# Token rows from grouped pairs of 64-column products, tokens dealt in two halves, one table set named first, and a new written order

## The chip, the cores and the metric

The kernel runs on one NeuronCore of a Trainium2 chip. The core has five engines that work side by side: TensorE (PE, with its weight loads shown apart as PEld), VectorE (DVE), ScalarE (ACT), GpSimd (POOL) and SyncE (SP, which issues most transfers). PE writes to PSUM, which DVE and ACT read. The metric is device time in microseconds, the lower the better: the median of timed runs. The changed kernel is compared with the kernel before by such runs.

## The reference

One block of a sequential model, for 2048 tokens of 512 channels: a layer norm, a convolution along the tokens with a state-space kernel (128 complex modes for each channel), a skip, then a second layer norm pair and a two-layer perceptron.

```python
x = A_u                                    # 1 x 2048 x 512, bfloat16
h = x + A(layernorm(x))                    # mixer along the tokens
h2 = h + B(layernorm(h))                   # B norms once more, then the perceptron

# A, for each channel d:
K[d, l] = Re( sum_n C[d,n] * exp(dt[d] * A[d,n] * l) * dt[d] * B[d,n] )
y = irfft(rfft(u, 2L) * rfft(K, 2L))[:L] + u * Dskip

# B:
g = gelu(layernorm(x) @ w1 + b1)           # 512 -> 1376
return g @ w2 + b2                         # 1376 -> 512
```

## The kernel before, in words

The convolution is done by a two-step transform over the 2048 tokens (padded to twice that), written as matrix products. A token number is split into a partition p (128) and a row j (16), token = 16 p + j. The small first step (BD, line 844) goes over the partitions; its result `a` goes to DRAM (A_dram) and comes back with the axes exchanged (X). The large step is `xps` (lines 882 to 885). The kernel's spectrum `kfps` (line 930) is multiplied in by DVE (`pa`, `pb`, then X), the inverse large step is `zps` (lines 966 to 969), its result `z` is written to DRAM (Zd) and read back with axes exchanged (ZT), and the inverse small step multiplies ZT by the matrix D (`Dm` in profiles) and so makes the token rows `y`. Each half of the 512 channels (hh = 0 and 1) goes through this by itself, in eight groups k2 of frequencies.

The state-space kernel itself (`kps`) is made from exponentials (ACT, `Pt` and `Q` from `th`), sines (ACT, `s` and `sq` from PE's phases `pv` and `qv`) and their products (DVE). Its `samples` go to DRAM (`KD`, line 784) and come back as `kt` (line 794), five pieces, all of which `kfps` needs. ACT must load a table set before it can change between sines and exponentials; `logs` (line 127) names the set that has both Ln and Exp, an activation without a named set loads one by itself.

All of this is one list of operations, each with a number; `Sched.run` (line 161) goes through the table ORDER and issues them as it says, and the last two bits of an entry choose the engine where there is a choice (ACT or DVE for a copy out of PSUM, SP or POOL for a transfer). There is no planner at run time: every engine works its instructions off in the order in which they were issued, and an instruction that waits holds up all behind it on its engine, SP's and POOL's transfers too.

The token rows are made in three ways. `early_rows` (line 1132) makes the first channel half of rows j = 0 to 7: for each row an identity product that adds the residual x, then one product with D for each half h of the frequencies, 128 columns each, added in PSUM (`half_rows`, line 1110). `head_rows` (line 1020) makes the second channel half of rows 0 to 3 and takes the last frequencies directly from `z` by a widened matrix W (`yh`). In `mlp` (line 1194) `y_rows` makes rows 4 to 7 of the second half and `y_row` (line 1221) makes rows 8 to 15 with all 512 channels at once, between the up-projections of the quarter before.

`mlp` works on four quarters of four rows (512 tokens): 11 blocks of up-projection (`h1ps`, line 1260, with Gelu on ACT into hT), then `down` (line 1265): for each row 11 products into `o2ps`, one DVE addition of h into `ot`, one store. Statistics and roots of the norms are on DVE (`ve` to `r4y`). PE's PSUM here has three tags: `h1ps` (four banks), `yps` (two) and `o2ps` (two). The loads of the perceptron's weights (`late_loads`, line 1180) are issued by SP once a one-column ACT copy into their tile (line 1096) has been done.

Of the kernel before, what the change touches and what calls it, by code (L numbers as in the profile page):

```python
# [11 lines left out]
ALU = mybir.AluOpType  # L12
f32 = mybir.dt.float32
# [3 lines left out]
P = 128  # L17
# [64 lines left out]
def bc(ap, shape):  # L82
    return ap.to_broadcast(shape)

# [104 lines left out]
def prefix(nc0, S, K, cp, ct, c2):  # L189
# [41 lines left out]
    split = ((3, 15), (0, 7), (0, 1), (1, 1))  # L231
    bits = c2.tile([P, 4], i32, name="bits")
    for n, (sh, m) in enumerate(split):
        ts(nc, bits[:, n:n + 1], pi[:], sh, ALU.logical_shift_right, m, ALU.bitwise_and)
    pf = ct.tile([P, 4], f32, name="pf")
    nc.vector.tensor_copy(pf[:], bits[:])
    t1, q, odd, b1 = (pf[:, n:n + 1] for n in range(4))
# [9 lines left out]
    t1s = col(t1, 1.0 / 64, 0.0)  # L247
# [12 lines left out]
    ts(nc, mask[:], kf[:, 0:8], q, ALU.is_equal)  # L260
# [222 lines left out]
def params(nc, S, K, cp, pp, sc, cv, psp, raws, ldt, dtb, grb):  # L483
    T, S2, Z = {}, S.op, {}

    def step():
        for h in range(2):
            d = slice(HW * h, HW * h + HW)
            nc.scalar.activation(dtb[:, d].rearrange("p (j g) -> p g j", g=4), ldt[:, d].rearrange("p (g j) -> p g j", g=4), ACT.Exp)
# [530 lines left out]
def head_rows(nc, S, K, psp, cv, o_tail):  # L1020
    K.o_head = []
    for n in range(2):
# [32 lines left out]
        m = S.op("PE", 0.65, main, K.o_z[0:6] + K.o_r0[0:1] + [o_tail], acq="p")  # L1055
# [54 lines left out]
def half_rows(nc, K, out, hh, js, more=False):  # L1110
    for j in range(js.start, js.stop):
        if more:
            nc.tensor.matmul(out[:, j - js.start], lhsT=K.ident[:], rhs=K.X[:, j, hh, 0:HW], start=True, stop=False)
        for h in range(2):
            nc.tensor.matmul(out[:, j - js.start], lhsT=K.D[:, h], rhs=K.ZT[:, hh, h, j, :], start=(h == 0 and not more), stop=(h == 1))
# [16 lines left out]
def early_rows(nc, S, K, psp, z0, r0):  # L1132
    for n in range(2):
# [14 lines left out]
        m = S.op("PE", 1.35, mm, z0 + r0[n:n + 1], acq="p")  # L1148
# [41 lines left out]
def residual(q, K, xv, n):  # L1190
    q.dma_start(K.X[:, 4 * n:4 * n + 4, :, 0:HW], xv[:, 4 * n:4 * n + 4].rearrange("p j (h d) -> p j h d", h=2))


def mlp(nc, tc, K, w1, w2, b2, xv, ov):
    with tc.tile_pool(name="m_sb", bufs=1) as sb, tc.tile_pool(name="m_rot", bufs=2) as rot, tc.tile_pool(name="m_ps", bufs=2, space=PSUM) as ps1:
        hT = [sb.tile([P, NFC, 512], bf16, name=f"hT{n}") for n in range(2)]
        y2, y2T, mv, yps = {}, {}, {}, {}
# [23 lines left out]
        def y_row(tb, jj):  # L1221
            yp = yps[tb, jj] = ps1.tile([P, 1, 2, HW], f32, name="y2", tag="yps")
            for h in range(2):
                nc.tensor.matmul(yp[:, 0], lhsT=K.D[:, h], rhs=K.ZT[:, :, h, 4 * tb + jj, :], start=(h == 0), stop=(h == 1))  # L1224
# [68 lines left out]
        for fc in range(NFC):  # L1293
            up(0, fc, pairs[1])
            if fc in (1, 3):
                y_rows(1, fc // 2)
# [156 lines left out]
```

## Time and profile before

| what | value |
|---|---|
| timed runs | 261.05, 261.68, 262.22 us; median 261.68 |
| profiled execution | the page gives its span: 260.3 us |
| PE, DVE, ACT busy | 220.3, 203.3, 179.5 us |
| granted TensorE clock | 1.000 |
| moved by DMA | 33.61 MB, 129 GB/s in the mean |

The span runs from the first to the last instruction of the profiled execution; a timed run has the start and the end of the program around it. In the rows below, PE's matmuls are pipelined: one lasts longer than the step to the next, and only the step counts for a stream.

### The profile page before, as it was taken

How to read it: one execution, taken by the hardware profiler on the slowest of the kernel's cores; microseconds unless marked ns; L12 is line 12 of the kernel's file. 1: busy time of each engine (PE TensorE's matmuls, PEld its weight loads, DVE VectorE, ACT ScalarE, POOL GpSimd, SP SyncE). 2: the span in 40 equal slices, each digit the busy share in tenths (PEclk: the TensorE clock that was granted, in tenths of full speed). 3: DMA queues.
4: the chain of work that ended last, by engine and by line, in shares of the span. 5: the costliest groups of instructions: out<-in, count | busy, mean ns of one | idle time of the engine just before them, and what ended most of it. 6: DMA issues, size and time to landing. Idle time of an engine off the chain costs nothing.

```text
span 260.3 us, 4481 instructions
## 1 busy us (share of the span) xinstructions
PE 220.3 (85%) x1585; PEld 138.3 (53%) x1585; DVE 203.3 (78%) x447; ACT 179.5 (69%) x303; POOL 40.0 (15%) x104
## 2 busy tenths in 40 slices
PE   2899308765688797899999999968999999999994
PEld 2323102322276585567988888857744444444443
DVE  6999999998999999999688999975836754761022
ACT  6999999999999999998833565448604703612810
POOL 8922960000003000100560010010000000000000
PEclk9999999999999999999999999999999999999999
DMA  5802951967695910410189678969541033022001
GB/s 166 293 7 34 191 162 61 162 170 244 183 357 148 227 11 24 139 44 0 53 180 267 185 201 242 264 197 240 141 102 59 1 63 101 0 54 80 31 26 54
DMA packets 49442, 33.61 MB, mean 129 GB/s; under 512 B 22154, under 2 KB 47900, under 8 KB 49164
## 3 DMA queue, kind: packets, MB, share of 16 engines
q1 hardware_dynamic: 47676, 28.66, 41.8%
q0 software_dynamic: 1744, 4.68, 7.1%
q8 instruction: 12, 0.20, 0.3%
q14 instruction: 10, 0.08, 0.1%
HBM read 18.65 MB, written 11.26 MB: 115 GB/s over the span
## 4 chain that ended last, share of the span: by engine, by line
PE 43%; DVE 16%; ACT 6%; DMA 6%; issue 2%; POOL 0%; DVEq 0%; POOLq 0%; ACTq 0%
PE o2ps L1273 14%; PE h1ps L1260 12%; PE kfps L930 8%; DVE Pt L79 5%; DMA ZT<-Zd 4%; DVE Q L79 3%; DVE X L79 2%; PE kps L765 2%; ACT Pt L673 2%; DVE pa L79 2%; DVE pb L79 2%; ACT sq L142 2%; DMA Zd<-z 2%; DVE X L91 1%; PE y L1224 1%
## 5 line engine op out<-in xcount | busy, mean ns | idle before, releaser
L1263 ACT ACTIVATE hT<-h1ps,b_sb 128x512 bf16<-128x512 f32 (+3 forms) x55 | 31.9, 604 | 41.9 <-PE h1ps L1260 40.2
L1260 PE MATMUL h1ps<-y2T,wide 128*128 128x512 bf16 (+3 forms) x220 | 40.5, 336 | 0.6 <-DVE ve L75 0.6
L1273 PE MATMUL o2ps<-w_sb,hT 128*128 128x512 bf16 (+3 forms) x187 | 38.7, 366 | 0.0
L930 PE MATMUL kfps<-kt,M 128*128 128x256 bf16 x320 | 37.9, 273 | 0.0
L79 DVE TENSOR_TENSOR ot<-o2ps,h 128x512 bf16<-128x512 f32 (+1 forms) x17 | 11.0, 658 | 30.3 <-PE o2ps L1273 16.9
L930 PEld LDWEIGHTS <-M 128*128 128x128 bf16 x320 | 31.3, 98 | 4.9 <-issue 1.2
L1260 PEld LDWEIGHTS <-wide 128*128 128x128 bf16 (+1 forms) x220 | 21.8, 100 | 17.0 <-issue 0.8
L1273 PEld LDWEIGHTS <-hT 128*128 128x128 bf16 (+1 forms) x187 | 18.3, 98 | 19.7
L79 DVE TENSOR_TENSOR Pt<-s,Pt 128x512 bf16<-128x512 bf16 (+1 forms) x48 | 23.0, 510 | 0.9 <-ACT s L142 0.3
L844 PE MATMUL aps<-u,BD 128*128 128x512 bf16 x32 | 10.2, 407 | 15.2 <-DVE u L839 11.2
L89 ACT CAST z<-zps 128x1024 bf16<-128x1024 f32 (+1 forms) x15 | 14.8, 992 | 10.6 <-PE zps L969 10.6
L673 ACT ACTIVATE Pt<-th 128x256 bf16<-128x256 f32 x64 | 20.7, 401 | 0.0
L142 ACT ACTIVATE sq<-qv 128x1024 bf16<-128x1024 int16 x20 | 20.1, 1077 | 0.0
L142 ACT ACTIVATE s<-pv 128x1024 bf16<-128x1024 int16 x16 | 16.9, 1077 | 0.0
L89 ACT CAST a<-aps 128x1024 bf16<-128x1024 f32 x16 | 15.8, 1053 | 0.5 <-DMA A_dram<-a 0.5
L738 PE MATMUL qv<-RQ,PQ 128*128 128x512 bf16 (+1 forms) x64 | 11.6, 298 | 4.7 <-ACT a L89 1.6
L844 PEld LDWEIGHTS <-BD 128*128 128x128 bf16 x32 | 3.0, 99 | 21.6 <-DVE u L839 14.3
L91 DVE CAST X<-xps 128x1024 bf16<-128x1024 f32 x12 | 14.3, 1219 | 0.0
L79 DVE TENSOR_TENSOR h<-y,X 128x512 f32<-128x512 f32 x10 | 6.9, 686 | 8.6 <-PE y L1224 5.6
L79 DVE TENSOR_TENSOR Q<-sq,Q 128x1024 bf16<-128x1024 bf16 x20 | 13.0, 685 | 0.1
L681 ACT ACTIVATE Q<-th 128x256 bf16<-128x256 f32 x40 | 13.0, 401 | 0.0
L449 POOL DMA_DIRECT2D Dp<-Dd x24 | 11.9, 504 | 7.2 <-DMA Dd<-ds 6.9
(246 smaller groups left out, 446.9 us busy)
## 6 DMA issues: line engine op xcount, KB each, us to landing
A_dram<-a SPq DMA_DIRECT2D x16, 256.0 KB, 2.6
X<-A_dram SPq DMA_DIRECT2D x4, 1024.0 KB, 7.2
Zd<-z SPq DMA_DIRECT2D x15, 256.0 KB, 3.4
x<-in_A_u_dram SPq DMA_DIRECT2D x4, 512.0 KB, 6.9
ZT<-Zd POOLq DMA_DIRECT2D x8, 256.0 KB, 4.1
ZT<-Zd SPq DMA_DIRECT2D x8, 256.0 KB, 3.6
out_dram<-ot SPq DMA_DIRECT2D x15, 128.0 KB, 1.9
X<-in_A_u_dram SPq DMA_DIRECT2D x3, 512.0 KB
```

The costliest lines, as they stand in the source:

```text
L79: (nc.vector if e == "DVE" else nc.gpsimd).tensor_tensor(out, a, b, op)
L89: nc.scalar.copy(out, in_)
L91: nc.vector.tensor_copy(out, in_)
L142: nc.scalar.activation(out, v.bitcast(i16)[..., 0:2 * n:2], ACT.Sin, scale=S2PI / 65536)
L449: nc.gpsimd.dma_start(t[o::128 // cnt], bass.AP(row.tensor, row.offset + 1024 * kh, [[0, cnt], [1, 1024]]))
L673: nc.scalar.activation(K.Pt[:, 1, :, k, :], K.th[:, ds].rearrange("p (e g) -> p e g", g=4), ACT.Exp, scale=float(8 * k))
L681: nc.scalar.activation(K.Q[:, 1, :, m, :], K.th[:, ds].rearrange("p (e g) -> p e g", g=4), ACT.Exp, scale=float(OFFS[m]))
L844: nc.tensor.matmul(ps[:, h, :], lhsT=K.BD[:, h].rearrange("p a b -> p (a b)"), rhs=cell["u"][:], start=True, stop=True)
L930: nc.tensor.matmul(ps[:, k, c, :], lhsT=K.M[:, t, k0 + k, c, :], rhs=kt[:, t, :], start=((plain or c == 1) and t == 0), stop=(t == 4))
L1260: nc.tensor.matmul(pt[:fs, 0:n], lhsT=K.w1_sb[:, dc, fc * P:fc * P + fs], rhs=(y2T[tb][:, dc, js, :] if tb or js.start else K.y2T[:, dc]). ...
L1263: nc.scalar.activation(hT[tb % 2][:fs, fc, cols], pt[:fs, 0:n], ACT.Gelu_apprx_tanh, bias=K.b1_sb[:fs, fc:fc + 1], scale=1.0)
L1273: nc.tensor.matmul(pt[:], lhsT=h[:fs, fc, jj * P:(jj + 1) * P], rhs=K.w2_sb[:fs, fc, d], start=(fc == 0), stop=(fc == NFC - 1))
```

## The change

1. Tokens are dealt otherwise: partition 64 h + p holds the rows 32 p + 16 h + j. With the mask of the forward small step made for that, the inverse small step falls apart into two halves: output partitions 64 h to 64 h + 63 need only half h of the frequencies. So the two products with D of a row, each 128 columns wide and added up, become two of 64 columns, each into its own half of the PSUM partitions.
2. These pairs are grouped: in `half_rows` all identity products come first, then all pairs; `y_rows` and `y_row` are called once per quarter, behind the third up-block (fc == 2), for all rows. For four rows at a time, two take their PSUM from the `o2ps` tag.
3. Loads of x and stores of the result go by partition halves (more transfers of x, each half as large; stores of two rows at once, and the last stores half on ACT's queue). The residual load r0 is now by halves, so that early and head rows need both of its parts.
4. `step`, the first exponentials, calls `logs` first.
5. Four small DVE operations more at the start (three bits and one combination), for the new mask.
6. A new table ORDER.

```diff
+def half(h):
+    return slice(64 * h, 64 * h + 64)
+
+def dealt(x):
+    return x.rearrange("(p h j) d -> h p j d", h=2, j=16)
...
-    split = ((3, 15), (0, 7), (0, 1), (1, 1))
+    split = ((3, 15), (0, 7), (0, 1), (1, 1), (2, 15), (0, 3), (6, 1))
...
-    t1s = col(t1, 1.0 / 64, 0.0)
+    t1s = col(tk, 1.0 / 64, 0.0)
...
-    ts(nc, mask[:], kf[:, 0:8], q, ALU.is_equal)
+    stt(nc, tq, tq, 2.0, th, ALU.mult, ALU.add)
+    ts(nc, mask[:], kf[:, 0:8], tq, ALU.is_equal)
...
     def step():
+        logs(nc)
         for h in range(2):
...
 def half_rows(nc, K, out, hh, js, more=False):
+    for j in range(js.start, js.stop) if more else ():
+        nc.tensor.matmul(out[:, j - js.start], lhsT=K.ident[:], rhs=K.X[:, j, hh, 0:HW], start=((j - js.start) % 2 == 0), stop=False)
     for j in range(js.start, js.stop):
-        if more:
-            nc.tensor.matmul(out[:, j - js.start], lhsT=K.ident[:], rhs=K.X[:, j, hh, 0:HW], start=True, stop=False)
         for h in range(2):
-            nc.tensor.matmul(out[:, j - js.start], lhsT=K.D[:, h], rhs=K.ZT[:, hh, h, j, :], start=(h == 0 and not more), stop=(h == 1))
+            nc.tensor.matmul(out[half(h), j - js.start], lhsT=K.D[:, h, half(h)], rhs=K.ZT[:, hh, h, j, :], start=not more, stop=not more or j % 2 == 1)
...
-            yp = yps[tb, jj] = ps1.tile([P, 1, 2, HW], f32, name="y2", tag="yps")
+            yp = yps[tb, jj] = ps1.tile([P, 1, 2, HW], f32, name="y2", tag="o2ps" if jj > 1 else "yps")
             for h in range(2):
-                nc.tensor.matmul(yp[:, 0], lhsT=K.D[:, h], rhs=K.ZT[:, :, h, 4 * tb + jj, :], start=(h == 0), stop=(h == 1))
+                nc.tensor.matmul(yp[half(h), 0], lhsT=K.D[:, h, half(h)], rhs=K.ZT[:, :, h, 4 * tb + jj, :], start=True, stop=True)
...
-            if fc in (1, 3):
-                y_rows(1, fc // 2)
+            if fc == 2:
+                for n in range(2):
+                    y_rows(1, n)
...
-                    if tb < 3 and fc in (1, 3, 5, 7):
-                        y_row(tb + 1, fc // 2)
-                        sums_row(tb + 1, fc // 2)
+                    if tb < 3 and fc == 2:
+                        for jj in range(4):
+                            y_row(tb + 1, jj)
+                        for jj in range(4):
+                            sums_row(tb + 1, jj)
...
     for n in range(4):
-        nc.sync.dma_start(x[:, 4 * n:4 * n + 4], xv[:, 4 * n:4 * n + 4])
+        for h in range(2):
+            nc.sync.dma_start(x[half(h), 4 * n:4 * n + 4], xv[h, :, 4 * n:4 * n + 4])
...
+                for b in range(2) if last or r else ():
+                    q = nc.scalar if last and b else nc.sync
+                    q.dma_start(ov[b, :, j:j + 1, d] if last else ov[b, :, j - 1:j + 1, :], ot[half(b), :, d])
```

Three places of the new order. First SP's queue where the second channel half's samples go to DRAM and come back (KD_66 and kt are of that half, Zd_67 and ZT of the first half), before:

```order
L997 DMA Zd_67<-z 128x4x256 x3
L784 DMA KD_66<-samples 128x1x320 x3
L794 DMA kt<-KD_66 128x4x64
L997 DMA Zd_67<-z 128x4x256
L794 DMA kt<-KD_66 128x4x64 x3
L1015 DMA wide<-Ds 4x8x128 x4
```

and now:

```order
L1009 DMA Zd_67<-z 128x4x256 x3
L796 DMA KD_66<-samples 128x1x320 x4
L1007 DMA ZT<-Zd_67 16x8192
L1009 DMA Zd_67<-z 128x4x256
L806 DMA kt<-KD_66 128x4x64 x2
L1007 DMA ZT<-Zd_67 16x8192
L806 DMA kt<-KD_66 128x4x64 x3
L1027 DMA wide<-Ds 4x8x128 x4
```

One KD and one kt that POOL issued have come to SP, and two ZT stand between them. On PE, one group of eight zps that stood ahead of the first kfps with this kt now stands behind it.

Second, DVE at the turn into the second layer (`y_22..` are the early rows, `yh` the head rows, `y_237.` the scaled rows of which PE makes the transposed `tps`), before:

```order
L91 CAST z<-zps 128x512
L1146 BN_STATS st_1905<-y_2248 128x6 x4
L1146 BN_STATS st_1905<-y_2277 128x6 x4
L1046 BN_STATS st_1905<-yh 128x6 x2
L1053 BN_AGGR mv_1906<-st_1905 128x2 x2
L1046 BN_STATS st_1905<-yh 128x6 x2
L75 TENSOR_SCALAR y_2376<-h,mv_1906,rs_1907 128x256 x4
L91 COPY y2T_1909<-tps 128x512
```

and now:

```order
L101 CAST z<-zps 128x512
L1158 BN_STATS st_2239<-y_2254 128x6 x4
L1158 BN_STATS st_2239<-y_2285 128x6 x4
L1058 BN_STATS st_2239<-yh 128x6 x2
L1065 BN_AGGR mv_2240<-st_2239 128x2 x2
L76 TENSOR_SCALAR y_2378<-h,mv_2240,rs_2241 128x256 x4
L1058 BN_STATS st_2239<-yh 128x6 x2
L101 COPY y2T_2243<-tps 128x512 x2
```

The scaling has moved ahead of the second statistics of the head rows. The CAST is of the last `z` of all now; before it was of the last but one, and the last was on ACT.

Third, ACT at the same place, before:

```order
L1142 COPY h<-y_2248 128x4x256
L1142 COPY h<-y_2277 128x4x256
L89 CAST z<-zps 128x512
L1049 COPY h<-yh 128x2x256
L1096 CAST wide<-h 128x1
L1070 ACTIVATE rs_1907<-mv_1906,eps 128x2
L1071 ACTIVATE rs_1907<-rs_1907 128x2
```

and now:

```order
L1154 COPY h<-y_2254 128x4x256
L99 CAST z<-zps 128x512
L1154 COPY h<-y_2285 128x4x256
L1082 ACTIVATE rs_2241<-mv_2240,eps 128x2
L1083 ACTIVATE rs_2241<-rs_2241 128x2
L1061 COPY h<-yh 128x2x256
L1108 CAST wide<-h 128x1
```

The root `rs` stands ahead of the copy of h and of the one-column copy that lets the weight loads go.

More of the change, by code (lines that the diff above doesn't have):

```diff
@@ L230, in prefix @@
         at += n
-    split = ((3, 15), (0, 7), (0, 1), (1, 1))
-    bits = c2.tile([P, 4], i32, name="bits")
+    split = ((3, 15), (0, 7), (0, 1), (1, 1), (2, 15), (0, 3), (6, 1))
+    bits = c2.tile([P, 7], i32, name="bits")
     for n, (sh, m) in enumerate(split):
         ts(nc, bits[:, n:n + 1], pi[:], sh, ALU.logical_shift_right, m, ALU.bitwise_and)
-    pf = ct.tile([P, 4], f32, name="pf")
+    pf = ct.tile([P, 7], f32, name="pf")
     nc.vector.tensor_copy(pf[:], bits[:])
-    t1, q, odd, b1 = (pf[:, n:n + 1] for n in range(4))
+    t1, q, odd, b1, tk, tq, th = (pf[:, n:n + 1] for n in range(7))
     cols = ct.tile([P, 5], f32, name="cols")
@@ L1053, in total @@
                 nc.vector.bn_aggr(K.mv0[:, j, :], K.st[:, j].rearrange("p h s -> p (h s)"))
-        m = S.op("PE", 0.65, main, K.o_z[0:6] + K.o_r0[0:1] + [o_tail], acq="p")
+        m = S.op("PE", 0.65, main, K.o_z[0:6] + K.o_r0 + [o_tail], acq="p")
         i = [S.op(("PE", "NONE"), (0.65, 0.0), pause, [m, K.o_zs[5]]) for _ in range(1 + 2 * n)]
@@ L1146, in stats @@
                 nc.vector.bn_stats(K.st[:, j, 0, :], cell["y"][:, j - js.start])
-        m = S.op("PE", 1.35, mm, z0 + r0[n:n + 1], acq="p")
+        m = S.op("PE", 1.35, mm, z0 + r0, acq="p")
         s = S.op("DVE", 1.5, stats, [m], rel=[m])
@@ L1190, in residual @@
 def residual(q, K, xv, n):
-    q.dma_start(K.X[:, 4 * n:4 * n + 4, :, 0:HW], xv[:, 4 * n:4 * n + 4].rearrange("p j (h d) -> p j h d", h=2))
+    h, rows = n % 2, slice(8 * (n // 2), 8 * (n // 2) + 8)
+    q.dma_start(K.X[half(h), rows, :, 0:HW], xv[h, :, rows].rearrange("p j (c d) -> p j c d", c=2))
 def mlp(nc, tc, K, w1, w2, b2, xv, ov):
@@ L1196, in mlp @@
         hT = [sb.tile([P, NFC, 512], bf16, name=f"hT{n}") for n in range(2)]
-        y2, y2T, mv, yps = {}, {}, {}, {}
+        y2, y2T, mv, yps, ots = {}, {}, {}, {}, {}
         def root(tb, js):
@@ L1266, in down @@
             j, h = 4 * tb + jj, hT[tb % 2]
-            parts = 2 if tb == 3 and jj == 3 else 1
+            last = tb == 3 and jj > 1
+            parts = 2 if last and jj == 3 else 1
+            if last or jj % 2 == 0:
+                ots[0] = rot.tile([P, 1 if last else 2, 512], bf16, name="ot", tag="ot")
+            ot, r = ots[0], 0 if last else jj % 2
             for n in range(parts):
@@ L1273, in down @@
                     nc.tensor.matmul(pt[:], lhsT=h[:fs, fc, jj * P:(jj + 1) * P], rhs=K.w2_sb[:fs, fc, d], start=(fc == 0), stop=(fc == NFC - 1))
-                ot = rot.tile([P, 512 // parts], bf16, name="ot", tag="ot")
-                tt(nc, ot[:], pt[:], K.h[:, j, d], ALU.add)
-                nc.sync.dma_start(ov[j][:, d], ot[:])
+                tt(nc, ot[:, r, d], pt[:], K.h[:, j, d], ALU.add)
+                for b in range(2) if last or r else ():
+                    q = nc.scalar if last and b else nc.sync
+                    q.dma_start(ov[b, :, j:j + 1, d] if last else ov[b, :, j - 1:j + 1, :], ot[half(b), :, d])
         tiles(0)
@@ L1341 @@
     psp = front.enter_context(tc.tile_pool(name="ps", bufs=1, space=PSUM))
-    xv = x_dram.rearrange("(p j) d -> p j d", j=16)
+    xv = dealt(x_dram)
     early = ExitStack()
@@ L1414 @@
     S.group = None
-    r0 = K.o_r0 = [S.op(("POOL", "SP"), (0.8, 0.45), lambda e, n=n: residual(nc.gpsimd if e == "POOL" else nc.sync, K, xv, n), x0[2 * n:2 * n + 2], lat=3.0) for n in range(2)]
+    r0 = K.o_r0 = [S.op(("POOL", "SP"), (0.8, 0.45), lambda e, n=n: residual(nc.gpsimd if e == "POOL" else nc.sync, K, xv, n), x0[0:4], lat=3.0) for n in range(2)]
     K.o_early = []
@@ L1420 @@
     front.close()
-    mlp(nc, tc, K, B_w1, B_w2, B_b2, xv, out_dram.rearrange("(p j) d -> j p d", j=16))
+    mlp(nc, tc, K, B_w1, B_w2, B_b2, xv, dealt(out_dram))
     order.__exit__(None, None, None)
```

47 rows, old and new, of the table ORDER are left out of this document.

## The prediction

> **What bounds the kernel now.** I read the page's busy shares first, then the busy times in stretches, then the chain of waits in order of time, and last the timeline at the places that the change touches. The page:
>
> ```profile
> span 260.3 us, 4481 instructions
> PE 220.3 (85%) x1585; PEld 138.3 (53%) x1585; DVE 203.3 (78%) x447; ACT 179.5 (69%) x303; POOL 40.0 (15%) x104
> ```
>
> No engine is full on average, so the stages have different limits. Two stretches of 20 us (start:end, length, then busy time and count of PE, PEld, DVE, ACT, POOL, then PE clock, DMA share, GB/s):
>
> ```profile
> 100.00:120.00 20.00, 16.92 (x159) 11.63 (x157) 19.55 (x39) 19.49 (x22) 0.90 (x1) 1.00 0.23 66
> 140.00:160.00 20.00, 19.76 (x180) 17.41 (x179) 19.09 (x36) 10.52 (x12) 1.93 (x4) 1.00 0.74 215
> ```
>
> Up to about 123 us ACT and DVE are both full; afterwards PE is, with DVE close to it until 160. The chain of waits, in order of time, shows the hand-over and what holds PE later (start, length, what):
>
> ```profile
> 121.20 1.96 ACT sq L142 x2
> 123.20 1.92 PE kps L765 x48
> ...
> 172.50 9.30 DMA ZT<-Zd
> ...
> 182.45 0.87 PE h1ps L1260 x8
> ...
> 198.06 0.43 PE y L1224 x2
> 198.49 1.73 PE h1ps L1260 x8
> ```
>
> So three things count: when ACT's last sines let PE go at 123.2, whether PE waits after that, and how many streaming slots PE needs. A matmul with 256 moving columns takes 0.87/8 = 0.109 us of the stream, one with 512 takes 1.73/8 = 0.216.
>
> **Part 1, the table load and the small DVE work.** The start of the kernel:
>
> ```profile
> 2.09 0.34 DVE L180 TENSOR_SCALAR bits<-pi 128x1 int32<-128x1 int32 x4 [2.09 <-POOL pi L196]
> 3.53 0.24 ACT L142 ACTIVATE wb<-bw 128x32 bf16<-128x32 int16 x1 [1.52 <-DVE bw L180]
> 3.79 1.28 ACT L489 ACT_TABLE_LOAD   x1
> 5.08 1.34 ACT L489 ACTIVATE M<-M 128x256 bf16<-128x256 bf16 x2
> 6.44 1.28 ACT L129 ACT_TABLE_LOAD   x1
> 6.46 0.69 DVE L79 TENSOR_TENSOR th<-tps_are,M 128x512 f32<-128x512 f32 x1
> 7.74 1.33 ACT L681 ACTIVATE Q<-th 128x256 bf16<-128x256 f32 x4
> ```
>
> The change makes the load at 3.79 the logarithm's, so the one at 6.44 goes: 1.28 us less on ACT. But the next exponentials need th. Three more DVE bits (0.34/4 each, 0.25) delay wb, hence the load, the two exponentials and th, which then ends at 6.46 + 0.25 + 0.69 = 7.40. ACT gains 7.74 − 7.42 = 0.3; DVE, equally full, starts th 0.25 later. Bounds at 123 us: a loss of 0.3, if DVE alone decides, to a gain of 1.3, the whole load, if the rest of the new order removes the engines' small waits. I take **+0.5**, the middle. The four more loads of x cost SP at most four KD issues (0.74 each, part 2), and SP has nothing else to issue before 22 us, so they are hidden; without that cover it would be 3 us.
>
> **Part 2, SP's queue at 126 us.** This term speaks against the change. Second half's kernel samples go out to DRAM (KD) and come back (kt), and PE's kfps of that half need all five kt:
>
> ```profile
> 126.15 2.23 SPq L784 DMA_DIRECT2D KD<-samples  x3
> 126.42 0.57 POOL L784 DMA_DIRECT2D KD<-samples  x1 [20.09 <-DVE X L79]
> 130.91 1.68 SPq L794 DMA_DIRECT2D kt<-KD  x3
> 134.96 0.57 SPq L995 DMA_DIRECT2D ZT<-Zd  x1
> 136.77 3.00 PE L930 MATMUL kfps<-kt,M 128*128 128x256 bf16 x26
> ```
>
> By the rows for the two transfers, from issue to landing (first KD, then kt):
>
> ```profile
> DMA to landing us min/median/max: 2.3/2.3/2.3
> DMA to landing us min/median/max: 3.7/3.7/4.0
> ```
>
> Before: the last kt is issued at 130.91 + 2 × 0.56 = 132.0 and lands at 135.7, 1.1 before PE's 136.77. In the new order POOL has none of these: SP issues four KD (126.15 + 3 × 0.74: the last at 128.4, landed 130.7), a ZT and a Zd meanwhile, then two kt, a ZT, three kt at about 0.56 each: the last kt at 130.7 + 5 × 0.56 = 133.5, landed at 137.2. And PE asks sooner, for one group of eight zps (8 × 0.109 = 0.87) now stands behind the first kfps of this half: at 135.9. PE waits 1.3, and everything behind in its queue (zps, all kfps) with it; DVE and ACT wait for those. PE has no slack from there to 171 us, so it is lost: **−1.3**. Bounds: 0, if kt lands in KD's 2.3 (135.8), and worse as rival C prices it.
>
> **Part 3, the turn into the second layer.** Here the new order and the paired matmuls meet:
>
> ```profile
> 165.00 0.68 DVE L91 CAST z<-zps 128x512 bf16<-128x512 f32 x1
> 165.60 2.79 DVE L1146 BATCH_NORM_STATS2 st<-y 128x6 f32<-128x256 f32 x8
> 166.04 0.27 PE L969 MATMUL zps<-X,Rn 128*128 128x256 bf16 x1
> 166.82 0.59 ACT L89 CAST z<-zps 128x512 bf16<-128x512 f32 x1
> 170.56 0.37 SPq L1181 DMA_DIRECT2D wide<-in_B_w_dram  x1
> 171.34 0.76 DVE L1046 BATCH_NORM_STATS2 st<-yh 128x6 f32<-128x256 f32 x2 [1.41 <-PE yh L1038]
> 172.01 1.37 DVE L75 TENSOR_SCALAR y<-h,mv,rs 128x256 bf16<-128x256 f32 x4
> 174.76 3.65 PE L1260 MATMUL h1ps<-y2T,wide 128*128 128x256 bf16 x32 [0.61 <-DVE ve L75]
> 181.84 0.61 PE L1115 MATMUL y<-ZT,Dm 128*128 128x256 bf16 x4 [0.80 <-DMA ZT<-Zd]
> ```
>
> The scaling of the first two rows (172.01) no longer queues behind statistics for which DVE idled 1.41. But DVE now casts the last z before the eight statistics and waits for PE's last zps (end 166.31). Pairs at no gain: cast to 167.2, eight statistics to 170.0, two more 0.76, about 1.2 for aggregate and root: scaling at 171.9, and with 0.76 of statistics now between it and the transposed copies PE starts at 175.0, 0.2 late. Pairs at full gain (16 products in 8 slots, 0.87 earlier): PE starts at 174.1 or somewhat before, 0.7 early. I take **+0.5**, nearer the upper end, since loads fit (part 4).
>
> The PE wait of 0.80 at 181.84 was for the last ZT, which took 9.30 behind the weight loads that SP began at 170.56. Now the ACT copy that lets those go stands behind the root and a copy of h, so they start at about 171.5, while the last Zd, cast directly, goes 0.2 to 1.1 earlier than 167.41. ZT is issued first, and the products that need it are four matmuls (0.44) later in PE's order. I take the whole wait as gone, **+0.8**; kept, it is 0. What is late next is the tail of the up weights:
>
> ```profile
> wide<-in_B_w_dram SPq DMA_DIRECT2D x1, 608.0 KB, 4.3
> ```
>
> Issued at 171.5, it is there at 175.8; with PE starting at 174.3 the columns are asked for 24 matmuls (2.6) later, at 176.9. So 1.1 is in hand; if the load takes longer than 5.4, PE waits.
>
> **Part 4, the pairs.** Two 128-column products per row become two of 64 columns into separate halves of PSUM. Rows before of the products, their loads, and the only narrower load that follows the same weights:
>
> ```profile
> L1224 PE MATMUL y<-ZT,Dm 128*128 128x512 bf16 x16 | 4.8, 379 | 0.0
> L1224 PEld LDWEIGHTS <-Dm 128*128 128x128 bf16 x16 | 1.6, 98 | 1.9
> L1260 PEld LDWEIGHTS <-wide 128*96 128x96 bf16 x20 | 2.4, 123 | 1.2
> ...
> 18.20 0.63 PE L368 MATMUL v<-gb,si 1*128 1x512 bf16 x1
> 18.63 0.63 PE L368 MATMUL v<-row_k,si 1*128 1x512 bf16 x1
> 19.19 0.58 PE L625 MATMUL k<-M,ones 128*1 128x512 bf16 x1
> ```
>
> No row has 64 columns. A load of 64, scaled from the 96-column row, is about 0.082, so two (0.164) fit under one 512-column matmul (0.216). A change of column count shows once: 0.56 between 18.63 and 19.19 where 0.43 is the step, so at most 0.13, 0.26 for going in and out. A group of eight 512-column products (two groups: third and fourth quarter of the rows) costs 8 × 0.216 = 1.73 now; 4 × 0.216 + 0.26 = 1.12 if pairs overlap, 1.99 if not: +1.2 to −0.5 for both. I take **+0.9**: the loads fit and the switch price is an upper one. The 256-column group of the second quarter is bound by its loads, 4 × 0.164 + 0.26 = 0.92 against 0.87: 0, with +0.3 to −0.3 around it. The new wait, for the down-projection's PSUM in rows 3 and 4 of a group, is met by DVE while twelve up matmuls (12 × 0.216 = 2.6) run.
>
> [...]
>
> Stores: fewer, larger, and the last halves on two queues; 0, give or take 0.3.
>
> **Sum** against the profiled span: 0.5 − 1.3 + 0.5 + 0.8 + 0.9 = 1.4, so 258.9. The timed median, 261.68, lies 1.4 above the span; I carry that over: **260.3**.
>
> **Rivals.** A: kt is in time (landing in KD's time, or asked later) and pairs overlap fully: 1.0 + 0 + 0.7 + 0.8 + 1.2 = 3.7, so 258.0. For it: 1.1 us of slack before; against: the count of SP's issues. B, slower: PE runs the two halves one after the other. Then the 512 groups lose 0.5, the 256 group 0.3, the early groups, with two switches each, start the layer 0.7 late: 0.5 − 1.3 − 0.7 + 0.8 − 0.3 − 0.5 = −1.5, 263.2. It decides from a pair costing 0.43 on. For it: no row shows overlap of two matmuls; against: separate columns and separate PSUM halves. C: the ZT transfers ahead of kt hold it longer, as 9.30 shows one can be held; each 1 us beyond 137.2 is lost whole, and from 2.7 more the kernel is slower by over 0.5%. With 2 more: 262.3. Against: ZT ran beside kt before, too.
>
> **Chances.** Forecast 0.45, A 0.25, B 0.15, C 0.15. This measurement tells apart about 0.5% (1.3 us), and the forecast sits on that edge: its share is split 0.22 faster, 0.21 no change, 0.02 slower. With A all faster, B 0.04 / 0.11 and C 0.08 / 0.07 (no change / slower): faster 0.47, no change 0.33, slower 0.20. The forecast's own range is 259.3 to 261.3; the range over the cases, leaving out the far ends of A and B, is 257.6 to 262.6.
>
> **What would show it.** One table load fewer by 8 us and the first long exponentials near 7.4; a PE wait of 1 us or more ahead of the first kfps of the second half, on kt; no wait on ZT in the second layer; y products of one 512-column group within 1.1 to 1.4 us, second starts of a pair close behind the first. No wait on kt, or pairs 0.43 apart, would make the prediction wrong.

## The result

The changed kernel takes 272.6 us in the median (270.2 to 273.7), the kernel before 261.5 in the same comparison: a ratio of 1.041, with a 95% interval from 1.036 to 1.047. Forecast were 260.3 us in a range from 257.6 to 262.6. The profiled execution has a span of 270.7 us, 10.4 more than before. In experiment 2, one execution of each of the two runs lies more than 1.5% above that run's fastest and is left out of its time and ratio.

The page of the changed kernel (busy time and share by engine, then the TensorE clock in 40 slices of the span, 9 standing for 90% or more):

```profile
span 270.7 us, 4459 instructions
PE 221.6 (82%) x1570; PEld 138.1 (51%) x1583; DVE 203.2 (75%) x451; ACT 178.3 (66%) x302; POOL 35.2 (13%) x96
PEclk9999999999999979999995999979999999999999
```

PE works 1.3 us longer than before (221.6 against 220.3), some of it under a slower clock, and no other engine works longer, so nearly all of the 10 us are waits. And the clock row, all nines before, has three dents, near 98, 146 and 182 us. PE's timeline shows a wait for a transfer just ahead of each (start, length, what, and in brackets the idle time before it and what ended it):

```profile
93.60 1.54 PE L942 MATMUL kfps<-kt,M 128*128 128x256 bf16 x9 [2.72 <-DMA M<-Bd]
...
144.66 4.21 PE L942 MATMUL kfps<-kt,M 128*128 128x256 bf16 x19 [4.92 <-DMA kt<-KD]
...
178.87 0.38 PE L1043 MATMUL yh<-ZT,Dm 96*128 96x256 bf16 x2 [2.60 <-DMA ZT<-Zd]
```

The second also shows what the dent costs: 19 kfps in 4.21 us, where 20 took 2.35 before. Busy times by stretch, cut finely, give the borders of the three slow stretches (after the busy times: granted clock, DMA share, GB/s):

```profile
94.50:95.00 0.50, 0.50 (x5) 0.36 (x4) 0.50 (x2) 0.00 (x0) 0.00 (x0) 0.54 0.00 0
97.50:98.00 0.50, 0.50 (x4) 0.38 (x3) 0.00 (x0) 0.48 (x1) 0.00 (x0) 0.55 0.00 0
142.00:142.50 0.50, 0.00 (x0) 0.00 (x0) 0.50 (x2) 0.00 (x0) 0.00 (x0) 0.82 1.18 111
149.00:149.50 0.50, 0.50 (x6) 0.41 (x5) 0.50 (x1) 0.00 (x0) 0.00 (x0) 0.85 1.15 285
179.00:180.00 1.00, 1.00 (x10) 0.88 (x9) 0.00 (x0) 0.52 (x1) 0.00 (x0) 0.94 1.07 373
183.00:184.00 1.00, 1.00 (x10) 0.83 (x8) 0.64 (x4) 0.29 (x1) 0.18 (x1) 0.86 0.83 262
```

Between these borders the clock is 0.50: from 94.5 to 97.9, from 142.3 to 149.2 and from 179.9 to 183.3, that is 3.4, 6.8 and 3.4 us. In the first stretch ACT and DVE, which bound the kernel there, run dry (busy for 0.38 and 0.61 of its 3.4 us): their casts and products wait for PE's slow kfps.

**The first wait** begins in SP's queue. The last kt reads, the last transposing load R from M, and only then the two writes of the table's last row, for which the kfps wait:

```profile
85.77 2.48 SPq L806 DMA_DIRECT2D kt<-KD  x3
88.29 2.59 SPq L490 DMA_TRANSPOSE R<-M  x1
90.93 1.60 SPq L473 DMA_DIRECT2D M<-Bd  x2
```

**The second** begins on POOL, with the residual rows (`X<-in_A_u_dram`, 512 KB). From POOL's timeline, and from the transfers issued between 134 and 145 us (count, KB each, median us from issue to landing):

```profile
134.92 0.86 POOL L1204 DMA_DIRECT2D X<-in_A_u_dram  x1
```

```profile
X<-in_A_u_dram POOLq DMA_DIRECT2D x1, 512.0 KB, 9.0
kt<-KD SPq DMA_DIRECT2D x5, 64.0 KB, 8.3
```

Before, POOL issued the first residual load at 105.4, when the transfers' engines were idle (DMA share 0.00 from 105 to 105.5 us), and it landed in 5.3 us. It filled four rows and needed two products of the first half; as half loads each fills eight rows and needs four, and the fourth is done only at 124 us. POOL then has a memset and four small transfers ahead of it. So it fell among the kt reads, and the kt reads took 8.3 us instead of 3.7 to 4.0.

**The third** is the way of the last z that the head rows need. ACT's cast for it ends at 170.3; the chain of waits, in order of time, shows both transfers behind it:

```profile
170.32 3.44 DMA Zd<-z
173.77 4.85 DMA ZT<-Zd
178.63 0.25 issue
178.87 0.38 PE yh L1043 x2
```

What the change meant to do works. Groups of eight paired products of 256 and of 512 columns (chain of waits) last 0.56, 0.98 and 1.05 us:

```profile
194.21 0.56 PE y L1127 x8
...
210.47 0.98 PE y L1237 x8
...
230.50 1.05 PE y L1237 x8
```

No ZT wait stands ahead of the first of them, where 0.80 stood before. And ACT starts its long exponentials with one load less, at 7.19 instead of 7.74:

```profile
3.79 1.28 ACT L139 ACT_TABLE_LOAD   x1
5.08 1.35 ACT L501 ACTIVATE M<-M 128x256 bf16<-128x256 bf16 x2
7.19 1.95 ACT L685 ACTIVATE Pt<-th 128x256 bf16<-128x256 f32 x6 [0.76 <-DVE th L80]
```

### The profile page after: what moved, and what is told of

It is laid out like the page before. It is cut to its first block, busy times and chain, and to the rows that moved or that the text cites. A ratio compares the mean times of both kernels' runs of the same rounds, so it can differ in the third digit from the quotient of the medians.

```text
span 270.7 us, 4459 instructions
## 1 busy us (share of the span) xinstructions
PE 221.6 (82%) x1570; PEld 138.1 (51%) x1583; DVE 203.2 (75%) x451; ACT 178.3 (66%) x302; POOL 35.2 (13%) x96
## 4 chain that ended last, share of the span: by engine, by line
PE 45%; ACT 19%; DVE 15%; DMA 13%; issue 4%; SPq 3%; POOL 1%; DVEq 0%; ACTq 0%; POOLq 0%
PE o2ps L1290 14%; PE h1ps L1273 13%; PE kfps L942 9%; DMA X<-A_dram 4%; DVE Pt L80 3%; DMA kt<-KD 3%; ACT s L152 2%; ACT a L99 2%; ACT sq L152 2%; ACT Q L693 2%; DMA ZT<-Zd 2%; PE yh L1050 2%; DVE Q L80 2%; ACT Pt L685 2%; DVE five L80 2%
## 5 line engine op out<-in xcount | busy, mean ns | idle before, releaser
L942 PE MATMUL kfps<-kt,M 128*128 128x256 bf16 x320 | 41.6, 287 | 7.6 <-DMA kt<-KD 4.9
L1273 PE MATMUL h1ps<-y2T,wide 128*128 128x512 bf16 (+3 forms) x217 | 39.3, 336 | 1.4 <-DVE mv L1065 1.2
L942 PEld LDWEIGHTS <-M 128*128 128x128 bf16 x320 | 32.6, 102 | 14.7 <-issue 6.4
L99 ACT CAST z<-zps 128x1024 bf16<-128x1024 f32 (+1 forms) x14 | 13.5, 987 | 16.3 <-PE zps L981 16.3
L750 PE MATMUL qv<-RQ,PQ 128*128 128x512 bf16 (+1 forms) x64 | 11.3, 298 | 4.0 <-ACT s L152 2.0
L80 DVE TENSOR_TENSOR X<-pa,pb 128x512 bf16<-128x512 bf16 (+1 forms) x34 | 12.4, 405 | 0.7
```

The costliest lines, as they stand in the source:

```text
L80: (nc.vector if e == "DVE" else nc.gpsimd).tensor_tensor(out, a, b, op)
L99: nc.scalar.copy(out, in_)
L942: nc.tensor.matmul(ps[:, k, c, :], lhsT=K.M[:, t, k0 + k, c, :], rhs=kt[:, t, :], start=((plain or c == 1) and t == 0), stop=(t == 4))
L1273: nc.tensor.matmul(pt[:fs, 0:n], lhsT=K.w1_sb[:, dc, fc * P:fc * P + fs], rhs=(y2T[tb][:, dc, js, :] if tb or js.start else K.y2T[:, dc]). ...
```

## Experiment 1: the order, or the rest

Theory: the three waits come from the new order of the transfers. Rival: pairs, half loads or the early table load are themselves slow.

```diff
 ORDER = [ the table of the kernel before, with
-    ... 2460, 1732 ...
+    ... 2025, 2460, 2328 ...
```

The entry 2460 is POOL's residual load, 2025 the ZT behind which it now stands; at its old place the rows it overwrites are still needed.

> The changed kernel with the order of the kernel before; one entry has to move, the first load of the residual rows, which now covers eight rows instead of four and so may only be issued once four products of the first half are done: it is put late on POOL, behind the ZT transfer that POOL issued at 142.6 us before. Theory 'the order': the three waits of PE in the changed kernel (2.72, 4.92 and 2.60 us, each with a stretch at half clock behind it) come from the order of the transfers, so all three go and the rest of the change shows its own price, a gain: early groups 0.56 instead of 0.87 each and two 512-column groups near 1.0 instead of 1.73 give 0.6 + 1.4 = 2.0, so 259 to 260 us, granted clock 1.00. Rival 'the rest': pairs, half loads and the earlier table load are themselves at fault, and the time stays above 265.

Measured: 260.8 us, ratio to the kernel before 0.995 (0.992 to 0.998). No wait on kt or M, and 0.40 on ZT ahead of the head rows. The rest of the change is a gain of about 1.3 us (0.5%); by the two ratios the order costs 4.6%, some 12 us. The 2.0 us expected are not reached, and the clock of the profiled execution is 0.993 and not 1.00; experiment 6 shows where it is lost.

Two more runs splice the orders where the samples of the second half are done:

```diff
+front = {the first 475 entries of the old order}
+new_front_old_back: [new order, entries in front] + [old order, the others]
+old_front_new_back: [old order, entries in front] + [new order, the others]
```

> The changed kernel's code; the steps up to the samples of the second half (475 entries, up to about 123 us) in the new order, all later steps in the order of the kernel before. It holds the first wait (table row behind the transposing loads, M<-Bd) and not the other two. By the changed kernel's trace the samples of the second half end 3.6 later than before (129.7 against 126.1): 260.8 + 3.6 to 4.2 = 264.4 to 265.0. If the front costs nothing once the rest is in the old order: 261.

> The reverse: the old order up to the samples of the second half, the new order for all later steps. It holds the waits on kt and on ZT ahead of the head rows, without the first. By the changed kernel's trace, 272.6 less 3.6 to 4.2, 268.4 to 269.0; with the front's share so taken, front and back add up to the whole. If the waits behind come only because the front is late against the transfers: 262 or less.

Measured: 265.2 us (1.012; 1.008 to 1.015) and 267.1 (1.018; 1.012 to 1.024). Against the 0.995 of the old order that is 1.7% (4.4 us) for the front and 2.3% (6.0) for the back; added up, 1.035, a little short of the changed kernel's 1.041 (1.036 to 1.047). PE's timelines of the two, in this order, hold the waits that each half should hold, and no other of more than 1.3 us past 86 us:

```profile
93.48 2.10 PE L942 MATMUL kfps<-kt,M 128*128 128x256 bf16 x9 [2.73 <-DMA M<-Bd]
```

```profile
141.27 3.27 PE L942 MATMUL kfps<-kt,M 128*128 128x256 bf16 x19 [4.13 <-DMA kt<-KD]
...
174.53 0.38 PE L1043 MATMUL yh<-ZT,Dm 96*128 96x256 bf16 x2 [2.16 <-DMA ZT<-Zd]
```

So the two parts are nearly independent, and the back loses time without the new front. Its 6 us are rough, though: the four executions lie between 264.9 and 268.8. In the profiled one the samples are 1.6 us later than with the old order, although up to there the order is the same: ACT's cast waited 1.1 us for a write of A_dram, PE 1.47 for that cast (to 59.92 us), and the clock row stands at 0.7 in the slice from 59.7 to 66.3 us: six aps took 2.74 us from 61.04, where the execution of the old order has four in 1.32 and a nine in the row. So 4.8 of that execution's 6.4 us arise behind the samples. The milestones of single executions, from the timelines (us):

| | before | changed | old order, new rest | new front | new back |
|---|---|---|---|---|---|
| second half's samples copied (ACT) | 126.1 | 129.7 | 125.5 | 129.3 | 127.1 |
| last zps starts (PE) | 166.0 | 175.9 | 165.0 | 168.8 | 172.0 |
| first up matmul (PE) | 174.8 | 187.2 | 174.1 | 177.9 | 181.5 |
| last addition into ot starts (DVE) | 257.0 | 267.2 | 255.2 | 259.2 | 261.6 |
| span | 260.3 | 270.7 | 258.8 | 263.0 | 265.2 |

## Experiment 2: the engine that issues, or the place

The prediction charged the move of transfers from POOL to SP. The move without the places, and the places without the move:

```diff
 ORDER: last two bits of 312, 318, 454, 460 (KD, kt) and 485, 492, 506, 533, 561 (ZT), and of 588 (ZT)
+old_order_new_queues: the nine on SP, 588 on POOL; places of the kernel before
+new_order_old_queues: the nine on POOL, 588 on SP; places of the changed kernel
```

> The run 'old_order_new_rest' (order of the kernel before) with only the issuing engine taken from the changed kernel: two KD writes, two kt reads and five ZT that POOL issued go to SP, and one ZT from SP to POOL; their places in the order stay. By the prediction's second term (too many issues on SP at 126 us) it loses 1.3, 262.1 against 260.8. If a ZT that waits on SP for its Zd also holds back what stands behind it there, more: two or three such stands of 1 to 3 us, 263 to 266. If the engine that issues has no part in it and only the place in the order counts: within 0.5 of 260.8.

> The changed kernel with only the issuing engine taken from the kernel before: the same ten transfers back on POOL (one ZT back on SP); the order stays. If the move to SP is what costs, most of the 10 us come back: 262 to 265. If the places in the order cost (the table row behind the transposing loads, the residual load among the kt, the late last z of the second half), the three waits of PE stay and so does the time, 270 to 273.

Measured: 263.2 us (1.003; 1.000 to 1.007), and 271.5 (1.035; 1.029 to 1.040). The move costs about 2.2 us (1.003 against 0.995 of 262.2; by the two intervals between 1 and 3.3), though not where the prediction had it: PE does not wait for kt in that run, but 1.6 us on ZT ahead of the head rows. The two profiled executions already stand 1.4 us apart at 66 us, ahead of anything that was moved. That is the same wait on A_dram as in the execution of the new back (1.1 us on ACT, 1.50 on PE, then six aps in 2.74 us and 0.7 in the clock row from 59.0 to 65.6), so that much of their distance is not the move's. With the old engines in the new order the time stays: PE waits 2.99 on the table row, 2.24 on ACT's z and 3.68 on ZT ahead of the head rows. The places carry the loss.

## Experiment 3: two single repairs of the new order

```diff
 table_row_before_turns (576 writes M from Bd, 612 is the last R from M)
-612, 1372, 1480, 1504, 1452, 1385, 1377, 1500, 616, 576,
+576, 612, 1372, 1480, 1504, 1452, 1385, 1377, 1500, 616,
 residual_after_kt (2460 is the residual load on POOL, 2061 POOL's next ZT)
-2460, 2104, 2112, ... 2056, 2061,
+2104, 2112, ... 2056, 2061, 2460,
```

> The changed kernel; on SP the two writes of the last table row (M from Bd) go ahead of the last transposing load R from M (2.59 us) instead of behind it. Theory 'queue on SP': they are issued at 88.3 instead of 90.9 and land near 91.0, so PE's wait of 2.72 at 93.6 falls to about 0.4, the clock stays whole until 98, ACT and DVE do not run dry: 2.3 + 1.7 = about 3.9 less, 268 to 269.5 us. Rival: the wait goes over to the last kt transfer, which lands as late; then the time stays within 1 us of 272.

> The changed kernel; on POOL the first load of residual rows (512 KB, issued at 134.9, in the middle of the kt transfers) goes behind the next ZT transfer of POOL (151.4). Theory 'contention': the last kt then lands in 3.7 to 4.0 us as before instead of 8.1, at about 141.0; PE's wait falls from 4.92 to about 1.5, too short for the half clock behind it: 3.4 + 2.2 = 5.6 less, 266 to 267.5 us. Rival 'SP's queue' (the term of the prediction with ZT ahead of kt as what holds it): the residual load has no part in it, kt lands after 8 us again and the time stays near 272.

> The changed kernel with both moves: the table row's writes ahead of the last transposing load, and the residual load behind the kt transfers. If the two stalls are independent, the gains add: 272 - 3.9 - 5.6 = 262 to 263.5 us, with the wait of 2.60 on ZT ahead of the head rows and its half clock still there. If the time of one stall is only taken up by the next, it stays above 266.

Measured: 269.1 us (1.023; 1.016 to 1.030), 270.6 (1.031; 1.026 to 1.037), and both together 269.7 (1.028; 1.024 to 1.033). By the ratios the first brings 1.8% (4.8 us, 3.9 expected), the second 1.0% (2.6 of the 5.6 expected), and together they bring 1.3%: the gains do not add. PE's timeline with the residual load moved, and the transfers issued there between 132 and 142 us:

```profile
139.90 2.23 PE L942 MATMUL kfps<-kt,M 128*128 128x256 bf16 x19 [0.45 <-DMA kt<-KD]
...
160.18 0.27 PE L978 MATMUL zps<-X,R 128*128 128x256 bf16 x1 [2.76 <-ACT z L99]
```

```profile
kt<-KD SPq DMA_DIRECT2D x5, 64.0 KB, 3.8
```

The theory of contention is borne out for this wait: the kt reads land in 3.8, PE waits 0.45 instead of 4.92. But 2.76 of it comes back 20 us later. ACT's z waits for a buffer (3.31, on Zd), because SP stands between two issues (from 141.7 to 147.7 and from 151.6 to 159.6 us). The residual load now stands at 147.3, ahead of the Zd that follow from 149.6; what it costs them was not tried:

```profile
140.51 1.15 SPq L1009 DMA_DIRECT2D Zd<-z  x2
147.66 1.81 SPq L1007 DMA_DIRECT2D ZT<-Zd  x3
149.57 2.01 SPq L1009 DMA_DIRECT2D Zd<-z  x3
159.57 1.14 SPq L1007 DMA_DIRECT2D ZT<-Zd  x2
```

The ZT at 147.66 waits for a Zd that SP issued just before it; the next Zd stand behind. The table row's repair, too, shortens its wait only to 2.16, now on the last kt, and the half clock behind it stays (0.50 from 94 to 96 us). So its gain is not the one that was expected: the samples come 1.1 us earlier, and the third stretch at half clock is gone (the clock row has nines from 147 us on; the ZT wait ahead of the head rows is 1.80 instead of 2.60). With both repairs the first wait of the profiled execution is 2.73 and is put down to the last kt.

## Experiment 4: ZT away from SP

If SP's stands on ZT are the cause of what is left, the ZT should go from POOL:

```diff
 ORDER of both_moves: last two bits of the ZT entries that choose (478 to 579)
-SP
+POOL
```

> The run 'both_moves' with the ZT transfers issued from POOL instead of SP, order of each queue kept. In 'both_moves' SP stands from 141.5 to 147.6 on a ZT that waits for the Zd issued just before it, and from 151.3 to 158.9 again; the Zd writes behind it are late, ACT's z waits for a buffer (3.0) and PE for PSUM (2.49), then for ZT (3.4). Theory 'SP's queue': with ZT on POOL the Zd writes go out when z is there; the PE waits of 2.5 and most of 3.4 go, and the half clock behind the latter: 6 to 7 less, 262 to 264 us. Rival 'the DMA engines are simply full': the Zd land as late, and the time stays above 267.

Measured: 271.4 us (1.035; 1.031 to 1.038). The theory falls as a remedy. The z wait of PE halves (1.24), but the wait ahead of the head rows grows from 3.4 to 6.5 us. The rows of SP, POOL and PE, one fence each:

```profile
164.47 0.98 SPq L1177 DMA_DIRECT2D wide<-in_B_w_dram  x2
```

```profile
168.62 0.48 POOL L1007 DMA_DIRECT2D ZT<-Zd  x1 [2.88 <-DMA Zd<-z]
```

```profile
176.20 0.58 PE L1043 MATMUL yh<-ZT,Dm 96*128 96x256 bf16 x2 [6.54 <-DMA ZT<-Zd]
```

SP, no longer held by ZT, issued 768 KB of weights 4 us ahead of the ZT that PE needed, which then took 7.3 us to land. That the weights are what slowed it was not tried by itself.

## Experiment 5: the parts of the rest

```diff
 old_order_full_columns: half_rows as before, and in y_row
-    nc.tensor.matmul(yp[half(h), 0], lhsT=K.D[:, h, half(h)], ..., start=True, stop=True)
+    nc.tensor.matmul(yp[:, 0], lhsT=K.D[:, h], ..., start=(h == 0), stop=(h == 1))
 old_order_log_late: in step
-    logs(nc)
 old_order_residual_by_rows: order before unchanged, in residual
-    h, rows = n % 2, slice(8 * (n // 2), 8 * (n // 2) + 8)
+    rows = slice(4 * n, 4 * n + 4)
+    for h in range(2):
 and in what the first two loads wait for
-    x0[0:4]
+    x0[2 * n:2 * n + 2]
```

> The run 'old_order_new_rest' with the paired products undone: each product of D again over 128 columns and both products of a row into the same PSUM rows (the halves of D that the pairs leave out are zero). Theory 'pairs overlap': 2 x 0.31 in the early rows, 2 x 0.7 in the third and fourth quarter and 0.3 in the second come back, so 2.0 to 2.3 slower than that run, 262.5 to 263.2 us against 260.8. [...]

> The run 'old_order_new_rest' without the early load of the logarithm's table: the exponential's load comes back at 3.8 us and the logarithm's behind it, as before. By the prediction's first term it is 0.5 slower (bounds 0.3 faster to 1.3 slower), 261.3 us against 260.8; the first long exponentials start near 8.4 instead of 7.18, since the three additional operations on DVE stay. Rival: ACT's gain is not handed on, because DVE sets the pace up to 123 us; no difference.

> The changed kernel with the order of the kernel before unchanged: the residual rows are loaded four at a time (two loads of 256 KB, one for each half of the partitions) instead of eight rows of one half, so the first load needs two products of the first half, not four, and may start at 105 us as before, when the DMA engines are idle. Theory 'the place of the load costs': 512 KB less in the full stretch 130 to 160, the ZT wait of 0.4 at 165.7 goes, 0.3 to 0.8 faster than 'old_order_new_rest', 260 to 260.5. Rival: at its late place the load hurts nothing in the old order, same time within 0.3.

Measured: 262.8 us (1.002; 1.000 to 1.005), 261.6 (0.994; 0.991 to 0.997) and 261.0 (0.997; 0.995 to 0.999), beside 260.8 (0.995; 0.992 to 0.998) with all parts. The pairs are worth 0.7%, 2 us. The early table load and the place of the residual load in the old order make no difference that these runs can tell: the rival held in both. Without the pairs the rest of the change is level with the kernel before.

## Experiment 6: the clock

Matmuls on constants where PE waits, never longer than the wait; everything else as in the changed kernel.

```diff
 ahead of a spectrum's products (22 for the first of hh = 0, 42 for the first of hh = 1)
+    nc.tensor.matmul(ps[:, 0, 1, :], lhsT=K.ident[:], rhs=K.top[:, 0:HW], start=True, stop=True)
 behind the first identity product of the head rows (20)
+    nc.tensor.matmul(o, lhsT=K.zero[:], rhs=K.D[:].rearrange("p h m -> p (h m)"), start=False, stop=False)
```

> The changed kernel with matmuls on constants put where PE waits, into PSUM that the next matmul overwrites or that gets zero added: 22 ahead of the first kernel spectrum of the first half (wait 2.72), 42 ahead of that of the second (wait 4.92), 20 behind the first identity matmul of the head rows (wait 2.60), 0.109 us each, so 2.4, 4.6 and 2.2 us, none of them longer than the wait. Nothing else differs: transfers, order and waits stay. Theory 'idle PE loses its clock': the three stretches at half clock (94.5 to 98.0, 142.3 to 149.1, 180.0 to 183.1) go, which is 1.7 + 2.2 + 1.6 = 5.5 less, 266.5 to 268 us, clock 1.00. Rival: the half clock has another cause (the 64-column matmuls, or load), it stays, and the time stays at 272 or a little above.

Measured: 267.3 us (1.020; 1.016 to 1.023), clock 1.000 in the profiled execution, 0.975 without the fillers. So about half of the 11 us (5.3 by the medians, 5.6 by the ratios) are not the waits themselves but the half clock behind them. The filler of the second wait in PE's timeline; the kfps behind it run at full step:

```profile
136.89 4.75 PE L938 MATMUL kfps<-top,ident 128*128 128x256 bf16 x42
141.48 2.35 PE L944 MATMUL kfps<-kt,M 128*128 128x256 bf16 x20
```

The same at the turn into the second layer, where PE has three short waits (0.73, 0.63, 0.61 us) and the profiled execution of experiment 1 lost its clock (0.87 from 170 to 175 us, 0.79 from 175 to 180):

```diff
 idle():   -for i in range(2):      +for i in range(5):
 turned(): behind the transposes
+    for i in range(5):
+        nc.tensor.matmul(K.spare[:, i % 2, 0:HW], lhsT=K.ident[:], rhs=K.top[:, 0:HW], start=True, stop=True)
```

> The run 'old_order_new_rest' with PE's short waits at the turn into the second layer filled with matmuls on constants (0.109 us each): ten instead of four ahead of the first transposes (idle there: 0.6 busy, then 0.73 waiting), and five behind each group of transposes (0.54 in waits of 0.63 and 0.61). In that run 32 up matmuls took 5.12 us instead of 3.65 at a granted clock of about 0.8 between 170 and 180 us. Theory 'idle PE loses its clock': that stretch goes in all executions, 1.0 to 1.5 less, 259.3 to 259.8 us. Rival: the fillers stand in the way of the copies and transposes, or the half clock comes anyway; within 0.4 of 260.8.

> The kernel before with the same fillers at the same place and nothing else. If the half clock at the turn also costs the kernel before in most executions (their clocks lie near 0.992), it gains about 1, 261.2 to 261.6 us against 262.3; the distance to the same fillers in the changed rest then stays at 1.5 to 2. If it has no such stretch, or the fillers cost, it stays within 0.3 of 262.3.

> The changed kernel with the order of the kernel before unchanged, residual rows loaded four at a time, and the fillers at the turn into the second layer. From the runs so far: 260.2 to 261.0 less what the fillers bring, 259.7 to 260.3 us, 0.9% less than the kernel before, its own interval clear of no change. Rival: the earlier residual load and the fillers do not add, and it stays at 260.8 to 261.

Measured: 260.2 us (0.991; 0.989 to 0.994), 262.0 (0.999; 0.997 to 1.001) and 259.5 (0.991; 0.988 to 0.995). With the changed rest the fillers bring 0.6 to 0.9, which is within what the two intervals leave open, and to the kernel before nothing certain. Two rows show what they prevent, the first 32 up matmuls in PE's timeline of the old order without fillers (3.65 us before), and the clock row on the page of the best version, which beats both kernels:

```profile
174.07 5.12 PE L1273 MATMUL h1ps<-y2T,wide 128*128 128x256 bf16 x32 [0.61 <-DVE ve L76]
```

```profile
PEclk9999999999999999999999999999999999999999
```

## Why the prediction was wrong

**The failed step is part 2.** It put PE's wait on kt at the right place and gave the sign by which to see it, but sized it by counting SP's issues: 1.3 us. The wait was 4.92. With the residual load out of the way, 0.45 of it is left in the new order (experiment 3). The other 4.5 come from a transfer that the prediction did not list: POOL's residual load, which as half loads needs four products and not two, and so goes from 105 to 135 us. Both facts stood in the sources, the dependence in the code (`x0[0:4]` for `x0[2 * n:2 * n + 2]`) and the place in the order; rival C had the mechanism (kt held by a transfer ahead) with the wrong transfer and at most a few us.

**A place was left out.** The prediction read SP's queue at 126 us alone. At 85 to 91 us the table row's writes had gone behind the last kt and a transposing load; the kernel was called full on ACT and DVE up to 123 us, and PE's waits there were taken as free. They are not when the wait ends in kfps that both engines need: the front cost 4.4 us. That its wait lies on the table row alone is not so (experiment 3: the last kt is as late); how the 4.4 us divide is not shown.

**Part 3** was right on the ZT wait in the second layer (gone, 0.80) and wrong on the start: PE came not 0.5 earlier but, counted from the last zps, 2.6 later (11.3 against 8.7 us from there to the first up matmul), since the ZT wait now stands ahead of the head rows. The prediction had followed the last z of all, which the head rows take directly, and not the last that comes back through DRAM.

**The clock had no term.** Its 5.3 to 5.6 us exceed every term of the sum. The kernel before had no wait of PE over 1.3 us past 60 us, and so no row that shows the price. In the changed kernel's trace the three stretches at 0.50, of 3.4, 6.8 and 3.4 us, come with waits of 2.72, 4.92 and 2.60 us; the second begins 2.6 us into its wait, the others 0.9 to 1.0 us after theirs. That a wait of 1.5 us would be too short for the half clock, as the expectation of 'residual_after_kt' has it, was the author's estimate; the wait left there was 0.45.

**Part 4** was right in mechanism and undersized. Forecast were +0.9 for the three groups, with 1.12 for a 512-column group and 0.92 for the 256-column one; measured 0.98, 1.05 and 0.56, against 1.73, 1.73 and 0.87: +1.7. A pair of 512 columns takes 0.25 to 0.26, not much above a single product's 0.216, so loads and products of the two halves do overlap. The load of 64 columns was undersized, 0.109 and not 0.082, and the 256-column group is not bound by its loads either: a pair takes 0.14, less than two loads one behind the other.

**Part 1**: the exponentials start 0.55 earlier (forecast 0.3), but the half microsecond at the end was not found (0.994 without the early load, 0.995 with it; the runs could not tell so little). **Stores**: from the last addition's end to the end of the span 3.1 us, 2.9 before, inside the 0.3 given.

Without part 2 the prediction's terms gave 2.7 less than before; with the old order 1.3 were measured. What remains open: how the back's 6 us divide between the kt wait, SP's stands and the late z, since each repair there moved the time to the next of them.

## What to carry to other kernels

A load that is regrouped inherits the latest of its new dependences: write down, for every transfer that a change touches, on any queue, when its data become free and what is in the transfers' way there. Where an order is rewritten, compare each queue over the whole program, not at the place that the change is about. And price a wait of TensorE with the half clock that may come with it (here 5.3 us for waits of 2.72, 4.92 and 2.60 us); constant matmuls in the waits took that part away here (267.3 us instead of 272.6).

## What was not expected of the hardware

- Whether a wait costs the clock is not a matter of its length alone. A wait of 2.16 us (table row moved, to 92.68 us) was followed by a stretch at 0.50 (94 to 96 us); one of 2.16 in the execution of the new back was not (to 174.53; 1.00 from 150 to 185), nor was one of 2.76 (residual load moved, 157.4 to 160.2; 1.00 from 155 to 170). At the turn three waits of 0.73, 0.63 and 0.61 us between 171.0 and 174.1 us were followed by 0.79 from 175 to 180 us in the execution of the old order with the new rest; waits of 0.73, 0.64 and 0.61 at the same place in that of the kernel before were not (1.00 from 170 to 185). What decides between these cases is not shown.
- The granted clock in the rows reads 1.00 from the start (in each of four stretches up to 44 us), yet there 512 columns take a step of 0.43 us, twice the later 0.216, though PE is busy (first the stretch, then products of the changed kernel before and after 44 us):

```profile
14.00:28.00 14.00, 13.66 (x37) 4.53 (x37) 13.63 (x36) 13.78 (x27) 0.80 (x3) 1.00 0.23 37
```

```profile
25.64 0.63 PE L379 MATMUL v<-gb,si 1*128 1x512 bf16 x1
26.07 0.63 PE L379 MATMUL v<-row_k,si 1*128 1x512 bf16 x1
...
41.91 1.74 PE L856 MATMUL aps<-u,BD 128*128 128x512 bf16 x4
```

```profile
50.03 0.27 PE L379 MATMUL v<-gb,ones 1*128 1x256 bf16 x1
50.14 0.27 PE L379 MATMUL v<-gb,si 1*128 1x256 bf16 x1
...
51.21 1.03 PE L856 MATMUL aps<-u,BD 128*128 128x512 bf16 x4
```

  The step is 0.22 again from about 44 us (two aps in 0.59 us at 44.63, one lev in 0.38 before). The shape (one row of weights) is not the reason: four products with all rows took 1.74 and later 1.03 us, and products with one row and 256 columns step by 0.11 at 50 us, the full pace. So PE ran at half pace in a stretch whose rows say 1.00; why, no run here shows. Some executions list a mean clock of 0.93 to 0.94 and are no slower than the others (waits filled: 267.4 us at 0.936 beside 267.2 at 0.999), as if some 34 us of half pace were counted there (an estimate: twice 0.064 of 265.6 us); that it is this start is not shown. The prediction took its price for a change of column count (0.13) from this stretch.
